# Folding the key weights of a linear-attention and FFN kernel in sixteen 32 by 32 array tiles, with block transpositions on VectorE in place of ScalarE copies

## The chip, the cores and the metric

The kernel runs on one NeuronCore of a Trainium2 chip. The metric is the device time of one execution in microseconds (us). Three executions of the kernel before took 513.17, 512.70 and 510.85 us, a median of 512.7. Beside these, one execution was profiled.

## The reference

A sigmoid gate, one number for each row of x, mixes two branches over the same input x of 2048 rows by 512 columns. Branch A is linear attention with 32 heads of 16 columns: queries and keys go through a small matrix per head (`w_phi`), then through a softmax of the result and one of its negative. Branch B is a feed-forward net with a squared ReLU. All is fp32.

```python
g = sigmoid((x * gate_w).sum(-1, keepdims=True))
q, k, v = split_heads(x @ wqkv)                       # 32 heads of 16
pq, pk = q @ w_phi[h], k @ w_phi[h]                   # per head
phi_q = concat(softmax(pq), softmax(-pq)); phi_k = concat(softmax(pk), softmax(-pk))
kv, z = phi_k.T @ v, phi_k.sum(rows)
a = (phi_q @ kv) / (phi_q @ z + 1e-6) @ wo
b = relu(x @ w1 + b1) ** 2 @ w2 + b2
out = g * a + (1 - g) * b
```

Since `x @ wk` is followed at once by `w_phi`, the kernel multiplies the two weight matrices first ("folds" them): `wk` (512 by 512) times a matrix that holds the 16 by 16 blocks of `w_phi` on its diagonal. Only the folded key weights, not the keys, are ever formed.

## The kernel before

**Precision.** Each fp32 product of the main work is three matmuls in a faster type: every operand is split into a high part (`hi`, a rounded copy, mostly by ScalarE) and a low part (`lo`, the difference, by VectorE), and `mm3` (L75 to L79) adds high by high, high by low and low by high. A matmul of this kind streams 512 columns. The fold is done in plain fp32 instead; there one matmul of the program gives two records in the trace.

**The FFN is the clockwork.** Its 14 chunks of 128 hidden columns run in two sweeps of seven over four blocks of 512 rows, 56 steps in all. A step is an `up` (12 matmuls into one PSUM bank `u`, then ReLU, square and split into `hh` and `hl`) and a `down` (12 matmuls, three for each of the four banks `d`). `up` runs two steps ahead of `down` (`LAG`). Each step has four slots, 2t, 2t + 0.5, 2t + 1 and 2t + 1.5; the last one stands between the second and the third `d` of a step. All attention work is hung into slots through `at(slot, function)`. The code sets the order in which work is offered; the scheduler orders each engine's queue by priority, `high_priority` pulls work ahead and `issue_after` fixes an order of two instructions.

**PSUM.** Four of the eight banks belong to `d`. The other four rotate: `bank()` hands out the one that was handed out longest ago, whoever asks: an `up`, a fold, a projection. A bank is written anew only when its last reader is done.

**Key and value weights.** Four tiles `raw[0]` to `raw[3]` of 128 by 1024 hold, for each quarter of the 512 input rows, the folded key weights beside the value weights; `raw[1]` and `raw[3]` lie in a tile named `tmp`. The value weights come by DMA (`joint_start`, L176); the folded ones come from PSUM. `joint(j, piece)` then makes of them the operands of seven products (the keys and values are computed by a scheme with seven block products in place of eight): subtractions on VectorE, and a split of each operand, into tiles named `slot...` and `w...`. Operands 1, 3 and 6 are stored to DRAM (`wkeep`) and loaded again later into the three slots by ScalarE's DMA queue (`again`, L556). The products `pX` and `pY` begin in slot 14 and read these operands.

**The fold.** `whole(k)` (L178 to L185) takes one bank, makes four 128 by 128 by 128 matmuls into its four quarters (input columns k of the transposed `wk`, held in four `row` tiles, by the diagonal `w_phi` matrix, in a fifth), and ScalarE copies the bank into `raw[k]` (L185). `joint(0, 0)` in slot 5 calls it for k = 0 and 2, `joint(1, 0)` in slot 6 for k = 1 and 3; after this one of the four banks (`ps_b`) leaves the rotation.

**Loads.** Weights and x come by SyncE's queue, which works in order. Weight and x tiles share four buffers (`stage`, tag `in`); a load waits until the split of the tile before it in that buffer is done. The gate's x tiles use the six `row` buffers, five of which hold the fold's inputs until the folds are done.

Of the kernel before, what the change touches and what calls it, by code (L numbers as in the profile page):

```python
# [10 lines left out]
AF = mybir.ActivationFunctionType  # L11
# [5 lines left out]
P = 128  # L17
S, D, H, DH, F = 2048, 512, 32, 16, 1792
NK = D // P
# [10 lines left out]
AHEAD = 150  # L30
# [5 lines left out]
def tile_gated_mix(ctx: ExitStack, tc: tile.TileContext, xT, xn, wqT, wkT, wphi, wv, wo, w1, b1, w2, b2, gw, out):  # L36
    nc = tc.nc
# [16 lines left out]
    def bank(name):  # L54
        p = banks[0]
        used(p)
        return p.tile([P, 512], F32, tag="s", name=name)
# [63 lines left out]
    st, up_w, down_w = {}, {}, {}  # L121
# [53 lines left out]
            st["raw"][k] = r  # L175
            nc.sync.dma_start(two(r)[:, :, 256:], two(wv[k * P:(k + 1) * P, :]))  # L176

    def whole(k):  # L178
        wph, *t = st["wT"]
        two = lambda a: a.rearrange("p (h c) -> p h c", h=2)  # L180
        ps = bank(f"fold{k}")
        for g in range(NK):
            nc.tensor.matmul(ps[:, g * P:(g + 1) * P], t[g][:, k * P:(k + 1) * P], wph[:, g * P:(g + 1) * P],
                             start=True, stop=True)
        nc.scalar.activation(two(st["raw"][k])[:, :, :256], two(ps), AF.Copy)  # L185

    def operand(i, j, src, slot=None, ehi=None, elo=None):
        if i in HELD:
# [9 lines left out]

    def joint(j, piece):
        raw, sub = st["raw"], lambda eng, o, a, b: eng.tensor_tensor(o, a, b, ALU.subtract)  # L200
        if piece == 0:
            whole(j)
            whole(2 + j)
        a, b = both(raw[j])
        c, d = both(raw[2 + j])
        if piece == 0:
            operand(3, j, d, j)
            operand(1, j, a, j)
            sub(nc.vector, a, b, a)
            sub(nc.vector, b, d, b)  # L210
        elif piece == 1:
            operand(5, j, a)
            operand(2, j, c)
            sub(nc.vector, a, d, a)
        else:
            operand(6, j, a, None if j else 2)
            sub(nc.vector, c, c, a)
            operand(7, j, b)
# [219 lines left out]
    def do_joint(j, piece):  # L438
        if (j, piece) == (0, 0):
            joint_start(st["wT"])  # L440
        with tc.issue_after(st["up"].ins):
            joint(j, piece)
        if (j, piece) == (1, 0):
            banks.remove(ps_b)
# [263 lines left out]
            at(2 * (fc - LAG) - 2, do_w1_first, fc)  # L708
        at(2 * (fc - LAG) - (2 if fc == LAG + 1 else 1), do_w2, fc)
    at(0, do_wT, wkT)  # L710
    for slot, j, piece in ((5, 0, 0), (6, 1, 0), (8, 0, 1), (9, 1, 1), (10, 1, 2), (11, 0, 2)):
        at(slot, do_joint, j, piece)
    for j in range(2):
        at(14.5, joint_last, j)
# [29 lines left out]
    for p in range(NB * NC // 2):  # L744
        n, s = 2 * p, 56.5 + 6 * p
        q, late = divmod(n, NC)[0], p == NB * NC // 2 - 1
# [13 lines left out]
    hid, last = {}, len(work_list) - 1  # L760
# [98 lines left out]
```

## Time and profile before

| | |
|---|---|
| three executions | 510.85, 512.70, 513.17 us |
| profiled execution, its time | 511.04 us |
| its span in the trace | 509.3 us (1.7 us lie around it) |
| granted TensorE clock | 0.999 |
| VectorE busy | 403.5 us (79%) |
| ScalarE busy | 254.8 us (50%) |
| fold of the key weights | PE 26.2 to 32.7 us, two blocks of 16 records |
| copies of L185 on ScalarE | 27.7 to 33.3 us, four of about 0.59 us |
| first `pX` | 54.31 us |

Times in rows of the trace are microseconds from the start of the span. A row of the timeline gives the start, the length, the engine, the line of the kernel, the operation, output and input tiles, the shape and the number of records merged; idle time of that engine before it stands in brackets with what ended it. A matmul's length includes its way through the array, so neighbours overlap, and what one costs is the distance between two starts: 0.227 us for the 512-column matmuls.

### The profile page before, as it was taken

The page shows a single profiled execution, that of the slowest core. Times are in us where ns is not written, and L with a number is a line of the kernel's source. Part 1 is how long each engine was busy: PE and PEld are TensorE (multiplying, and loading weights), DVE is VectorE, ACT ScalarE, POOL GpSimd, SP SyncE. Part 2 cuts the span into 40 slices and gives each one's busy share as a digit, 9 for nine tenths or more (in the row PEclk, how much of TensorE's full clock was granted, in tenths as well). Part 3 has the DMA queues.
Part 4 walks back from the last instruction along what each step waited for, and adds up shares of the span by engine and source line. Part 5 has one row for each costly group of instructions (what it writes and reads, how often), then busy time and mean ns, then how long its engine had stood idle before and what let it go on. Part 6 is the DMA issues. An engine that isn't in the chain of part 4 may idle for free.

```text
span 509.3 us, 9129 instructions
## 1 busy us (share of the span) xinstructions
PE 502.8 (99%) x3421; PEld 408.0 (80%) x3421; DVE 403.5 (79%) x668; ACT 254.8 (50%) x445; POOL 91.0 (18%) x106
## 2 busy tenths in 40 slices
PE   8999999999999999999999999999999999999997
PEld 4888888888788888788888878788787878788775
DVE  3559848888884979796998989897969797897723
ACT  4778645556253565463564744444456354333540
POOL 1001640204320024000012140211222120111200
PEclk9999999999999999999999999999999999999999
DMA  8975696667844478762266131324112231032112
GB/s 256 324 247 186 231 325 194 200 210 226 291 167 142 171 237 288 281 208 83 73 198 228 50 96 40 106 72 143 48 32 85 69 88 47 3 120 68 37 27 83
DMA packets 46628, 76.12 MB, mean 149 GB/s; under 512 B 6776, under 2 KB 23928, under 8 KB 46584
## 3 DMA queue, kind: packets, MB, share of 16 engines
q1 hardware_dynamic: 35544, 41.58, 26.5%
q10 hardware_dynamic: 8224, 24.51, 13.8%
q0 software_dynamic: 2816, 9.45, 5.1%
q8 instruction: 27, 0.44, 0.3%
q14 instruction: 17, 0.14, 0.1%
HBM read 57.68 MB, written 11.54 MB: 136 GB/s over the span
## 4 chain that ended last, share of the span: by engine, by line
PE 93%; DVE 3%; DMA 3%; issue 0%; DVEq 0%; ACT 0%
PE d L77 10%; PE d L78 9%; PE d L79 9%; PE u L77 9%; PE u L78 9%; PE u L79 9%; PE att L79 3%; PE att L78 3%; PE q L78 3%; PE q L77 3%; PE att L77 3%; PE q L79 3%; PE pX L579 3%; PE pX L577 2%; PE pX L578 2%; PE pY L577 2%
## 5 line engine op out<-in xcount | busy, mean ns | idle before, releaser
L407 ACT ACTIVATE r<-u,b1c 128x512 f32<-128x512 f32 x56 | 38.5, 687 | 125.3 <-PE u L79 123.8
L77 PE MATMUL d<-w2h,hh 128*128 128x512 f32 x224 | 87.8, 392 | 0.0
L78 PE MATMUL d<-w2l,hh 128*128 128x512 f32 x224 | 87.3, 390 | 0.0
L79 PE MATMUL d<-w2h,hl 128*128 128x512 f32 x224 | 87.2, 389 | 0.0
L77 PE MATMUL u<-xh,w1h 128*128 128x512 f32 x212 | 83.8, 395 | 0.0
L78 PE MATMUL u<-xl,w1h 128*128 128x512 f32 x212 | 82.6, 390 | 0.0
L79 PE MATMUL u<-xh,w1l 128*128 128x512 f32 x212 | 82.5, 389 | 0.0
L322 POOL TENSOR_TENSOR ez<-e,z 128x512 f32<-128x512 f32 x32 | 42.8, 1358 | 165.9 <-ACT e L294 165.9
L67 DVE TENSOR_TENSOR hl<-r,hh 128x512 fp32r<-128x512 f32 x56 | 37.7, 674 | 23.7 <-ACT hh L64 23.7
L77 PEld LDWEIGHTS d<-w2h,hh 128*128 128x128 f32 x224 | 42.1, 188 | 9.1 <-issue 0.4
L78 PEld LDWEIGHTS d<-w2l,hh 128*128 128x128 f32 x224 | 42.1, 188 | 8.9 <-DVE w2l L67 0.4
L79 PEld LDWEIGHTS d<-w2h,hl 128*128 128x128 f32 x224 | 42.1, 188 | 8.8
L77 PEld LDWEIGHTS u<-xh,w1h 128*128 128x128 f32 x212 | 39.8, 188 | 11.0 <-issue 3.1
L79 PEld LDWEIGHTS u<-xh,w1l 128*128 128x128 f32 x212 | 39.8, 188 | 8.4
L78 PEld LDWEIGHTS u<-xl,w1h 128*128 128x128 f32 x212 | 39.8, 188 | 7.8
L297 DVE TENSOR_REDUCE sm<-e 128x64 f32<-128x1024 f32 x27 | 32.8, 1213 | 11.1 <-ACT e L294 11.1
L294 ACT ACTIVATE e<-e 128x1024 f32<-128x1024 f32 x27 | 28.6, 1059 | 25.0 <-DVE e L292 24.7
L64 ACT ACTIVATE hh<-r 128x512 fp32r<-128x512 f32 x56 | 35.1, 627 | 0.9
L408 ACT ACTIVATE r<-r 128x512 f32<-128x512 f32 x56 | 34.9, 624 | 0.8
L360 ACT ACTIVATE phiT<-tb 32x256 f32<-32x256 f32 x64 | 26.4, 412 | 6.1 <-DVE tb L345 5.1
L329 DVE TENSOR_REDUCE dz<-ez 128x64 f32<-128x1024 f32 x16 | 19.4, 1210 | 11.6 <-POOL ez L322 11.6
L616 ACT ACTIVATE tmp<-pX 128x512 f32<-128x512 f32 x24 | 14.3, 597 | 27.3 <-PE pX L579 27.3
(171 smaller groups left out, 982.2 us busy)
## 6 DMA issues: line engine op xcount, KB each, us to landing
sloto<-wkeep ACTq DMA_DIRECT2D x30, 512.0 KB, 4.2
in<-in_xT SPq DMA_DIRECT2D x44, 256.0 KB, 3.7
slotez<-wkeep ACTq DMA_DIRECT2D x15, 512.0 KB, 4.5
phiT<-tb SPq DMA_DIRECT2D x192, 32.0 KB, 1.9
in<-in_w SPq DMA_DIRECT2D x23, 256.0 KB, 3.3
part<-row POOLq DMA_DIRECT2D x16, 256.0 KB, 5.0
row<-part SPq DMA_DIRECT2D x16, 256.0 KB, 3.1
out<-row SPq DMA_DIRECT2D x15, 256.0 KB, 2.2
```

Source lines behind the costliest of these rows:

```text
L64: i = nc.scalar.activation(hi, src, AF.Copy)
L67: st["lo"] = elo.tensor_tensor(lo, src, hi.bitcast(F32), ALU.subtract)
L77: nc.tensor.matmul(o, ah[:, sa], bh[:, sb], start=first, stop=False)
L78: nc.tensor.matmul(o, ah[:, sa], bl[:, sb], start=False, stop=False)
L79: return nc.tensor.matmul(o, al[:, sa], bh[:, sb], start=False, stop=last)
L294: nc.scalar.activation(ef, ef, AF.Exp)
L297: nc.vector.tensor_reduce(sm, e3, AX.X, ALU.add)
L322: nc.gpsimd.tensor_tensor(ez[:, hs, :], e3[:, hs, :], zbc[half], ALU.mult)
L360: nc.scalar.activation(dst, src, AF.Copy)
L407: st["relu"] = nc.scalar.activation(r, ps, AF.Relu, bias=b1c[:, fc:fc + 1])
L408: nc.scalar.activation(r, r, AF.Square)
L577: nc.tensor.matmul(ps, h, wh, start=first and j == 0, stop=False, skip_group_check=True)
```

## The change

`whole` goes. `tiles_fold` takes its place, once, in slot 5.5 in place of 5 and 6. It takes all four rotating banks at the same time and makes 64 matmuls of 32 by 32 (stationary: a 32 by 32 block of the diagonal `w_phi` matrix) by 128 columns (moving: the transposed `wk`). `r` picks the array's row tile and the bank, `c` its column tile, `g` the quarter of the bank; an order is fixed with `r` running fastest. The products are the same sums of 32 terms, of which 16 are not zero, but the result comes out transposed. So VectorE turns it: 16 block transpositions of 128 partitions by 128 elements, four per bank, straight from PSUM into the `raw` tiles, in a fixed order, bank by bank. The four copies on ScalarE are gone. Lines behind the change have moved by 11 to 14: L257 is now L268, L200 is L214, L577 is L590.

```diff
-    def whole(k):
-        wph, *t = st["wT"]
-        two = lambda a: a.rearrange("p (h c) -> p h c", h=2)
-        ps = bank(f"fold{k}")
-        for g in range(NK):
-            nc.tensor.matmul(ps[:, g * P:(g + 1) * P], t[g][:, k * P:(k + 1) * P], wph[:, g * P:(g + 1) * P],
-                             start=True, stop=True)
-        nc.scalar.activation(two(st["raw"][k])[:, :, :256], two(ps), AF.Copy)
+    def tiles_fold(loaded):
+        wph, *t = loaded
+        pss = [bank(f"fold{r}") for r in range(4)]
+
+        def mm(g, r, c):
+            rows, cols = slice(32 * r, 32 * r + 32), slice(32 * c, 32 * c + 32)
+            return nc.tensor.matmul(pss[r][cols, g * P:(g + 1) * P],
+                                    wph[rows, g * P + 32 * r:g * P + 32 * r + 32],
+                                    t[g][rows, :].rearrange("p (k c q) -> p k c q", c=4, q=32)[:, :, c, :],
+                                    start=True, stop=True, skip_group_check=True)
+
+        last = None
+        for x in [(g, r, c) for g in range(NK) for c in range(4) for r in range(4)]:
+            with tc.issue_after(last.ins) if last else nullcontext():
+                last = mm(*x)
+        turned = None
+        for r in range(4):
+            for k in range(NK):
+                src = pss[r].rearrange("p (h g k q) -> p h g k q", h=2, g=2, k=NK)[:, :, :, k, :]
+                dst = st["raw"][k].rearrange("p (h z g r f) -> p h z g r f", h=2, z=2, g=2, r=4)[:, :, 0, :, r, :]
+                with tc.high_priority(offset=AHEAD), tc.issue_after(turned.ins) if turned else nullcontext():
+                    turned = nc.vector.transpose(dst, src)
...
     def joint(j, piece):
-        if piece == 0:
-            whole(j)
-            whole(2 + j)
...
         if (j, piece) == (0, 0):
             joint_start(st["wT"])
+            with tc.issue_after(st["up"].ins):
+                tiles_fold(st["wT"])
...
-    for slot, j, piece in ((5, 0, 0), (6, 1, 0), (8, 0, 1), (9, 1, 1), (10, 1, 2), (11, 0, 2)):
+    for slot, j, piece in ((5.5, 0, 0), (6, 1, 0), (8, 0, 1), (9, 1, 1), (10, 1, 2), (11, 0, 2)):
```

How the queues of two engines change follows; `d_302` to `d_305` are the four banks of `down`, `w2h_262` and `w2h_268` the weights of the third and fourth step, `w1h_321`, `w1h_347` and `w1h_504` (before: `w1h_432`) the weights of the fifth, sixth and seventh chunk.

TensorE before, where the second half of the fold stands between a whole `down` and the `up` of the sixth chunk (the first half, `fold_397` and `fold_403`, stands right ahead of that `down`):

```order
L77 MATMUL d_305<-w2h_262,hh 128x512
L78 MATMUL d_305<-w2l_263,hh 128x512
L79 MATMUL d_305<-w2h_262,hl 128x512
L183 MATMUL fold_436<-row 128x128 x4
L183 MATMUL fold_442<-row 128x128 x4
L77 MATMUL u<-xh_0_145,w1h_347 128x512
L78 MATMUL u<-xl_0_146,w1h_347 128x512
```

TensorE after: the end of the 64 small matmuls, which now stand in one piece between the second and the third bank of that `down`. `fold_404` to `fold_407` are the four banks:

```order
L184 MATMUL fold_404<-row 32x128
L184 MATMUL fold_405<-row 32x128
L184 MATMUL fold_406<-row 32x128
L184 MATMUL fold_407<-row 32x128
L77 MATMUL d_304<-w2h_262,hh 128x512
L78 MATMUL d_304<-w2l_263,hh 128x512
L79 MATMUL d_304<-w2h_262,hl 128x512
```

TensorE after, ten rows behind the small matmuls (six for `d_304` and `d_305`, then these four), where the `up` of the sixth chunk begins:

```order
L77 MATMUL d_302<-w2h_268,hh 128x512
L78 MATMUL d_302<-w2l_269,hh 128x512
L79 MATMUL d_302<-w2h_268,hl 128x512
L77 MATMUL d_303<-w2h_268,hh 128x512
L77 MATMUL u<-xh_0_145,w1h_347 128x512
L78 MATMUL u<-xl_0_146,w1h_347 128x512
```

So the fold has moved six matmuls back, into one block, and four matmuls of the next `down` have moved ahead of the `up`; the other eight follow behind it, and then the `up` of the seventh chunk. The rotation gives that sixth `up` the bank `fold_405`, the second of the four, because the first leaves the rotation in between; it waits for VectorE's eighth transposition. The seventh `up` gets `fold_406`.

VectorE before, from the low part of the first x tile of the next block on:

```order
L67 TENSOR_TENSOR xl_0_459<-in,xh_0_458 128x512
L67 TENSOR_TENSOR sloto_388<-raw_393,sloto_388 128x512
L67 TENSOR_TENSOR xl_1_470<-in,xh_1_469 128x512
L67 TENSOR_TENSOR w_518<-raw_393,w_517 128x512
L67 TENSOR_TENSOR w2l_384<-in,w2h_383 128x512
L67 TENSOR_TENSOR sloto_389<-tmp,sloto_389 128x512
L67 TENSOR_TENSOR w1l_433<-in,w1h_432 128x512
```

VectorE after, the start of the transpositions behind the two x tiles:

```order
L67 TENSOR_TENSOR xl_0_519<-in,xh_0_518 128x512
L67 TENSOR_TENSOR xl_1_530<-in,xh_1_529 128x512
L199 STREAM_TRANSPOSE raw_398<-fold_404 128x2x2x32
L199 STREAM_TRANSPOSE tmp<-fold_404 128x2x2x32
L199 STREAM_TRANSPOSE raw_400<-fold_404 128x2x2x32
```

VectorE after, behind the last of them:

```order
L199 STREAM_TRANSPOSE tmp<-fold_407 128x2x2x32
L67 TENSOR_TENSOR w2l_384<-in,w2h_383 128x512
L67 TENSOR_TENSOR sloto_395<-raw_400,sloto_395 128x512
L67 TENSOR_TENSOR w1l_505<-in,w1h_504 128x512
L67 TENSOR_TENSOR sloto_396<-tmp,sloto_396 128x512
L67 TENSOR_TENSOR w_578<-raw_400,w_577 128x512
```

All 16 transpositions stand in one piece ahead of the splits of the next weights. The low part of the seventh chunk's weights, `w1l`, stands behind the split of a `raw` tile now, and so behind its high part on ScalarE. On every engine the order is the same again from the second `pX` on (about 67 us).

## The prediction

> **What bounds the kernel now.** I read the page first: the busy shares, then the chain that ended last by engine.
>
> ```profile
> span 509.3 us, 9129 instructions
> PE 502.8 (99%) x3421; PEld 408.0 (80%) x3421; DVE 403.5 (79%) x668; ACT 254.8 (50%) x445; POOL 91.0 (18%) x106
> PE 93%; DVE 3%; DMA 3%; issue 0%; DVEq 0%; ACT 0%
> ```
>
> The chain runs through TensorE for 93% of the span. So time is gained by taking work from TensorE's queue, and lost by a wait put into it. ScalarE is half idle: its four copies count only if something waits for them. Next comes the stage of the change, by the table of stages (columns: window, length, then busy time and records of PE, PEld, DVE, ACT and POOL, clock, DMA share, GB/s).
>
> ```profile
> 23.50:33.00 9.50, 9.50 (x59) 8.46 (x58) 5.58 (x10) 6.96 (x13) 0.57 (x1) 1.00 0.60 204
> 33.00:54.00 21.00, 21.00 (x94) 17.41 (x93) 17.78 (x32) 14.07 (x27) 4.45 (x6) 1.00 0.70 243
> ```
>
> TensorE has no gap here at full clock; VectorE is busy for 85% of the second window. Whatever goes onto VectorE can delay something. Last, TensorE's timeline around the fold.
>
> ```profile
> 26.00 0.39 PE L79 MATMUL u<-xh,w1l 128*128 128x512 f32 x1
> 26.23 1.95 PE L183 MATMUL fold<-row 128*128 128x128 f32 x16
> 27.93 0.48 PE L77 MATMUL d<-w2h,hh 128*128 128x512 f32 x1
> 28.25 0.40 PE L78 MATMUL d<-w2l,hh 128*128 128x512 f32 x1
> ...
> 30.75 1.95 PE L183 MATMUL fold<-row 128*128 128x128 f32 x16
> 32.45 0.48 PE L77 MATMUL u<-xh,w1h 128*128 128x512 f32 x1
> ...
> 37.99 0.39 PE L77 MATMUL u<-xh,w1h 128*128 128x512 f32 x1
> ...
> 38.44 0.39 PE L79 MATMUL u<-xh,w1l 128*128 128x512 f32 x1
> ```
>
> **Term 1, the fold on TensorE.** A block of 16 records holds the queue from 26.23 to 27.93, and the step to the next matmul is 0.32 in place of 0.23: 1.70 + 0.09 = 1.79. Two blocks: **3.58 us go**.
>
> The new block is 64 matmuls, 128 records at two each. The trace has no 32 by 32 tiles, but two relatives: L312 with four column tiles (the weight loads show its pace best) and L371 with two row by four column tiles.
>
> ```profile
> 111.27 0.39 PE L79 MATMUL d<-w2h,hl 128*128 128x512 f32 x1
> ...
> 111.59 0.61 PEld L312 LDWEIGHTS kvps<-e,vext 128*17 128x17 f32 x64 [0.35 <-DVE gate L264]
> 112.10 0.63 PEld L312 LDWEIGHTS kvps<-tmp,vext 128*17 128x17 f32 x64
> 112.78 0.19 PEld L577 LDWEIGHTS pY<-w,sh 128*128 128x128 f32 x1
> 112.89 0.19 PEld L578 LDWEIGHTS pY<-w,sh 128*128 128x128 f32 x1
> ```
>
> ```profile
> 492.07 1.09 PE L371 MATMUL num<-phiT,kvb 64*32 64x256 f32 x32
> 493.09 0.50 PE L77 MATMUL d<-w2h,hh 128*128 128x512 f32 x1
> ```
>
> L312 passes 128 records in 1.19 us (111.59 to 112.78), 9 ns each. Its neighbour would have followed 111.27 at 111.50, so 0.09 is lost on entry, and some 0.2 on leaving. Streaming alone is no higher: an old fold record takes 1.70/16 = 0.106 us, and 128 of them on 16 tiles are 0.85. I take L312's pace: 1.19 + 0.3 = **1.5 us come**. The ends: 0.85 + 0.3 = 1.15 below; above, L371's pace, 1.02 us for 32 records, so 4.1 + 0.3 = 4.4. TensorE's own work falls by about 2.1 us.
>
> **Term 2, the wait that is added.** The fold holds all four rotating banks, so the next `up`, ten matmuls behind it, waits for VectorE's eighth transposition. When do these begin? ScalarE and VectorE before:
>
> ```profile
> 27.15 0.63 ACT L408 ACTIVATE r<-r 128x512 f32<-128x512 f32 x1
> 27.69 0.58 ACT L185 ACTIVATE raw<-fold 128x512 f32<-128x512 f32 x1
> 28.16 0.62 ACT L64 ACTIVATE hh<-r 128x512 fp32r<-128x512 f32 x1
> ```
>
> ```profile
> 28.82 0.69 DVE L67 TENSOR_TENSOR hl<-r,hh 128x512 fp32r<-128x512 f32 x1 [1.61 <-ACT hh L64]
> 29.43 0.68 DVE L257 SCALAR_TENSOR_TENSOR row<-row,gwb 128x512 f32<-128x512 f32 x1
> ...
> 30.04 0.69 DVE L67 TENSOR_TENSOR xl<-in,xh 128x512 fp32r<-128x512 f32 x1
> ...
> 31.25 0.68 DVE L67 TENSOR_TENSOR xl<-in,xh 128x512 fp32r<-128x512 f32 x1
> ```
>
> The copy at 27.69 stood ahead of `hh`; without it `hh` starts when `r` is done, near 27.81, and `hl` near 28.47. Then come the gate's row and two x tiles at 0.605 each: the first transposition starts at 28.47 + 4 x 0.605 = 30.89, with the fold finished at 26.23 + 6 x 0.227 + 1.4 = 29.0. So not the fold but VectorE's queue sets the start. Price of one transposition of 128 elements from PSUM, which the trace doesn't have:
>
> ```profile
> 342.19 1.24 DVE L345 STREAM_TRANSPOSE tb<-e 128x1024 f32<-128x1024 f32 x1
> 343.35 0.65 DVE L289 TENSOR_REDUCE mx<-q 128x32 f32<-128x512 f32 x1
> ```
>
> ```profile
> 12.49 0.69 DVE L495 TENSOR_TENSOR w1l<-row,w1h 128x128 fp32r<-128x128 f32 x3
> 13.10 0.68 DVE L67 TENSOR_TENSOR w1l<-row,w1h 128x512 fp32r<-128x512 f32 x1
> ```
>
> ```profile
> L680 DVE COPY kvb<-kvt x4: 279/286/298, 258.1 to 261.1; 32x128 f32<-32x128 f32 x4
> ```
>
> Three operations of 128 elements take 0.61 from start to start, 0.20 each. The 1024-element transposition takes 1.16; ordinary ones go by 0.605 for 512 and 0.20 for 128, so 1.05 ns an element and 0.07 fixed, 1.14 for 1024. It costs 0.02 to 0.03 more, so 0.23 each. Lower end 0.20; upper end 0.29, the full length of a PSUM copy of 128 elements, if nothing overlaps; and, far off, 0.60, if small blocks cost what 512 elements cost. By 0.23 the eighth is done at 30.89 + 8 x 0.23 + 0.13 (the tail of the last and the signal) = 32.86. TensorE gets there at 27.59 + 1.5 + 10 x 0.227 = 31.36 and waits **1.5 us**. Its whole queue stands behind that wait: this `up`, the rest of the `down`, the seventh `up`; ScalarE's ReLUs wait for these, but their results are used two steps later.
>
> The Trainium skill, VectorE: DVE Perf Modes, The three transpose paths, gives 311 ns for a 128x128 bf16 transpose on VectorE. If that held from start to start, the eighth would be done at 33.5 and the whole change would come to -0.05 us, 511.1; the trace's 1.24 us long row starts its successor 0.08 before its end, so I hold that figure for a length.
>
> **Net.** The `up` after that starts 20 matmuls later, at 32.86 + 20 x 0.227 = 37.40; before, at 37.99. So **0.6 us** is gained (3.58 - 1.5 - 1.5, the same).
>
> **What else moves.** The seventh `up` needs `w1h` and, in its third matmul, `w1l`:
>
> ```profile
> 36.59 0.63 ACT L64 ACTIVATE w1h<-in 128x512 fp32r<-128x512 f32 x1 [1.94 <-DMA in<-in_w]
> 37.26 0.69 DVE L67 TENSOR_TENSOR w1l<-in,w1h 128x512 fp32r<-128x512 f32 x1 [1.80 <-ACT w1h L64]
> ```
>
> Its load waits for the second x tile's buffer. That tile was done at 31.93; now it is done at 30.97, so at the old latency the tile lands near 35.6, by 1.0 earlier. `w1l` now stands behind a high part (0.52) and a low part (0.6): 35.6 + 0.6 + 0.5 + 0.7 + 0.7 = 38.1 at worst, against a need at 37.40 + 0.45 = 37.85. SyncE's two gate loads now go ahead of it, but no store of a slot competes. I take no wait; bound 0.25. The sixteen transpositions take 3.7 and end at 34.7. VectorE idled 21.00 - 17.78 = 3.2 us in the window from 33 to 54, 1.80 of it right ahead of that `w1l`, so its backlog at the window's end is about the old one; if that cover were gone, the first `pX` would be late by 0.5 at most. ScalarE's four copies (the one above takes 0.58, so 2.3 us) I cost at nothing: it idles half the time.
>
> Around 56 to 77 us ScalarE's queue changes too: a reload of the first slot now stands behind a copy of `pX` that came at 66.07.
>
> ```profile
> 62.68 0.33 ACTq L565 DMA_DIRECT2D sloto<-wkeep  x1
> ...
> 66.07 0.60 ACT L616 ACTIVATE tmp<-pX 128x512 f32<-128x512 f32 x1 [2.28 <-PE pX L579]
> ...
> 70.25 0.33 ACTq L565 DMA_DIRECT2D sloto<-wkeep  x1
> ```
>
> ```profile
> 76.75 0.39 PE L577 MATMUL pX<-sloto,xh 128*128 128x512 f32 x1
> ```
>
> ```profile
> DMA to landing us min/median/max: 3.7/4.2/5.5
> ```
>
> ```profile
> 124.01 4.49 DMA sloto<-wkeep
> ```
>
> The line on landing counts the slot loads between 50 and 80 us; the last row is a piece of the chain. So this 512 KB load leaves 3.4 us later and lands by 71.6, beside POOL's loads, and still runs when the next one leaves at 70.25. That one is needed by `pX` at 76.75, and at 5.5 us has 1.0 left. I take 0; the far end is 0.6, all that was gained.
>
> **Sum.** 511.04 - 0.6 = 510.4 for the profiled execution. It lies 1.7 below the median of 512.7; the four known executions have their middle at 511.9. I predict 511.9 - 0.6 = **511.3**.
>
> **Rivals.**
> 1. *The gain is given back at the slot reloads.* For: the chain holds such a load, of 4.49 us, further on, and the moved one falls into busy traffic. Against: 1.0 us left. Time: no change, 511.9 (511.0 on the profile's basis).
> 2. *Slower: the transpositions cost more.* The deciding point is 0.305 us each (37.99 - 4.54 - 30.89 - 0.13, by eight); above it the bank wait outweighs the fold. For: block work straight from PSUM, unseen here. Against: 0.20 and 1.16. At 0.60 each the bank comes free at 35.8 (loss 2.4) and `w1l` is ready near 42.6 (loss 4.1): 516.0. The Trainium skill, TensorEngine Tiling (Array Packing), PSUM Bottleneck, says that tiles speed up TensorE and not the emptying of PSUM, which may become the bottleneck. By that rule this rival or the forecast's 1.5 us wait is what to expect; no run so far shows which.
> 3. *The tiles don't run side by side as hoped.* At L371's pace the block is 4.4: the fold ends at 31.9, the eighth transposition at 33.9, TensorE arrives at 34.3: loss 0.9, 512.8. One after another (128 x 0.106 = 13.6) would lose 10. Against: L371 does run eight tiles at once, 32 records of about 0.21 in 1.02.
> 4. *The wait doesn't bind* and the 2.1 us stay: 509.8. It would need transpositions that start 1.5 us earlier; nothing in the queue allows it.
>
> **How the numbers follow.** Chances: forecast (gain 0.3 to 0.9) 0.5; rival 1 0.22; rival 2 0.14, of which 0.05 dear enough for over 0.5%; rival 3 0.07; rival 4 0.07. About 0.5%, 2.6 us, is what a measurement of this kernel can tell from no change. Even the whole 2.1 is under it, so faster is left to rival 4 and a lucky scatter of the runs, 0.07; slower has 0.05 of rival 2, 0.02 of rival 3 and 0.03 of scatter, 0.10; the rest, 0.83, lies within. Low end: the fastest execution 510.85 less 1.2; high end: the slowest, 513.17, plus 0.7 for rivals 2 and 3: 509.6 to 513.9.
>
> **What would show it.** Right: one block of 128 fold records of 1.2 to 1.6 us; transpositions 0.2 to 0.3 apart from about 30.9; a TensorE gap of 1 to 2 us, released by VectorE, ahead of the sixth `up`; the seventh `up` at 37.2 to 37.7. Wrong: no gap there (rival 4), a gap at `w1l` or a step over 0.3 (rival 2), a fold block over 3 us (rival 3), a new gap at `pX` near 76 (rival 1).

## The result and the profile after

The changed kernel took 514.51 us (median of 7 runs, 513.54 to 516.17), the kernel before 511.47 (7 runs beside it, 510.85 to 513.17): ratio 1.0057, 95% interval 1.0043 to 1.0071, so **slower by 3.0 us**. 511.3 was predicted. The profiled execution of the changed kernel took 513.54, 2.5 more than that of before.

First the page of the changed kernel: span, busy times, the chain by engine, and the queue that brings instructions (packets, MB, share).

```profile
span 511.7 us, 9331 instructions
PE 502.2 (98%) x3517; PEld 405.4 (79%) x3517; DVE 406.2 (79%) x684; ACT 253.3 (49%) x441; POOL 91.4 (18%) x106
PE 68%; issue 13%; DVE 7%; DMA 5%; ACT 2%; POOL 2%; SPq 1%; DVEq 0%; POOLq 0%; ACTq 0%
q8 instruction: 28, 0.46, 0.4%
```

TensorE is busy for 0.6 us less, and the span is 2.4 longer: TensorE waits. Before, the chain ran through it for 93%; now for 68%. The page of before has 27 packets on the last line, not 28.

The waits of TensorE (total, times, longest), without those at the start and at `kvps`, which both kernels have:

```profile
PE d L77 <- DVE row L822: 1.6, 1, 1.6
...
PE pX L592 <- issue: 0.7, 1, 0.7
...
PE u L77 <- DVE tmp L199: 0.7, 1, 0.7
...
PE num L382 <- DMA phiT<-tb: 0.4, 1, 0.4
```

Only the third of these was forecast. The others lie at 61, 212 and 303 us. TensorE's and VectorE's timeline at the fold:

```profile
27.55 1.90 PE L184 MATMUL fold<-row 32*32 32x128 f32 x128
...
32.62 0.47 PE L77 MATMUL u<-xh,w1h 128*128 128x512 f32 x1 [0.67 <-DVE tmp L199]
...
37.25 0.39 PE L77 MATMUL u<-xh,w1h 128*128 128x512 f32 x1
```

```profile
30.77 0.31 DVE L199 STREAM_TRANSPOSE raw<-fold 128x128 f32<-128x128 f32 x1
...
33.78 0.27 DVE L199 STREAM_TRANSPOSE tmp<-fold 128x128 f32<-128x128 f32 x1
```

Here the change does what was forecast: the seventh `up` starts at 37.25 in place of 37.99. To see where the gain goes, the same matmul is followed through both traces. The table gives, for every profiled execution, how much later than in the first profile of before the same `down` matmul starts, as the growth of that offset in each stage; stages are named by their times in before. "Load" is when ScalarE starts the high part `w2h` near 34 us, which waits for a weight load. The kernels below the third row are explained with the experiments.

| profile | start | fold, 23 to 41 | 41 to 52 | block end, 52 to 71 | 71 to 194 | 194 to 249 | 249 to 325 | load |
|---|---|---|---|---|---|---|---|---|
| after | -0.13 | -0.60 | 0.00 | +1.96 | 0.00 | +0.49 | +0.75 | 33.80 |
| after_again | -0.07 | +0.08 | 0.00 | +2.23 | +0.19 | +1.36 | +0.74 | 35.12 |
| after_third | -0.12 | -0.24 | 0.00 | +2.09 | +0.76 | +1.51 | +0.27 | 34.51 |
| before_again | +0.71 | 0.00 | 0.00 | +0.02 | +1.05 | -0.19 | +0.05 | 34.20 |
| load_only | -0.06 | +0.08 | +1.44 | 0.00 | -0.07 | -0.14 | -0.28 | 35.62 |
| tile_only | -0.23 | -1.09 | +1.51 | +1.14 | +0.99 | +1.05 | +0.81 | 34.37 |
| order_back | -0.04 | -0.64 | 0.00 | +2.05 | +0.05 | +0.80 | +1.31 | 33.97 |
| later_w4 | +0.21 | -0.62 | 0.00 | +1.75 | -0.06 | +0.52 | +0.57 | 33.82 |
| old_order | -0.26 | -0.04 | 0.00 | +1.05 | +0.64 | +0.98 | -0.05 | 34.22 |
| less_vec | -0.06 | +0.72 | 0.00 | +1.45 | -0.07 | +1.06 | +0.50 | 35.73 |
| two_step_l | +0.53 | -1.44 | +1.13 | +0.65 | -0.07 | +3.29 | +0.68 | 34.43 |
| phase_after | +0.02 | +0.39 | +0.01 | +2.01 | +0.41 | 0.00 | -0.31 | 35.53 |
| mid_after | +0.56 | +0.30 | 0.00 | +1.85 | +0.96 | 0.00 | -0.32 | 35.83 |
| later_w4_phase | +0.63 | +0.08 | 0.00 | +1.24 | +0.50 | -0.52 | -0.11 | 35.79 |
| old_order_mid | -0.14 | -0.19 | 0.00 | +1.48 | +1.15 | -0.53 | -0.28 | 34.78 |
| two_step_lp | +0.11 | -0.79 | +1.42 | +0.69 | +0.49 | -0.46 | -0.28 | 35.02 |
| two_step_rp | +0.07 | -0.79 | +1.55 | +0.05 | +2.13 | +0.01 | -0.17 | 34.97 |
| phase_before | +2.29 | +0.02 | +0.11 | 0.00 | +0.30 | +1.24 | +0.85 | 35.95 |
| mid_before | +0.29 | 0.00 | 0.00 | 0.00 | +5.43 | +1.26 | +0.62 | 33.78 |

The first row sums to +2.5, the difference of the two times. One profile is one execution: between 71 and 194 us a second profile of the unchanged kernel loses 1.05, 0.7 of it a wait of `pX` for a slot reload, so only what comes back in several profiles is read here. The gain at the fold, 0.60, was predicted at 0.59. It is lost three times over at the end of the first block, and some more at two places where the engines' orders are the same in both kernels.

**The block end.** There VectorE finishes the gate (L268 to L276) and then adds the first `d` banks to the output (L822), which frees them for the next block's `down`. VectorE and ScalarE after:

```profile
54.12 0.69 DVE L268 SCALAR_TENSOR_TENSOR row<-row,gwb 128x512 f32<-128x512 f32 x1
54.73 0.09 DVE L268 DVE_READ_ACCUMULATOR row<-row,gwb 128x1 f32 x1
54.73 1.22 DVE L67 TENSOR_TENSOR hl<-r,hh 128x512 fp32r<-128x512 f32 x1
55.87 1.22 DVE L67 TENSOR_TENSOR w<-raw,w 128x512 fp32r<-128x512 f32 x1
57.02 0.70 DVE L274 TENSOR_SCALAR gate<-gate 128x4 f32<-128x4 f32 x1
57.63 0.68 DVE L67 TENSOR_TENSOR w<-tmp,w 128x512 fp32r<-128x512 f32 x1
58.23 0.16 DVE L275 RECIPROCAL gate<-gate 128x4 f32<-128x4 f32 x1
58.43 0.50 DVE L276 TENSOR_SCALAR rest<-gate 128x4 f32<-128x4 f32 x1
58.85 1.45 DVE L67 TENSOR_TENSOR sl<-in,sh 128x512 fp32r<-128x512 f32 x2
60.22 0.75 DVE L822 SCALAR_TENSOR_TENSOR row<-d,rest,row 128x512 f32<-128x512 f32 x1
```

```profile
56.63 0.60 ACT L629 ACTIVATE tmp<-pX 128x512 f32<-128x512 f32 x1 [1.58 <-DMA wkeep<-spare]
57.72 0.63 ACT L64 ACTIVATE sh<-in 128x512 fp32r<-128x512 f32 x1 [0.49 <-POOL in L560]
58.94 0.63 ACT L64 ACTIVATE sh<-in 128x512 fp32r<-128x512 f32 x1 [0.59 <-POOL in L561]
59.48 0.71 ACT L813 ACTIVATE row<-b2b,rest 128x512 f32<-128x512 f32 x1
```

From the end of the gate's row (54.81) to the end of the first evacuation (60.97) pass 6.2 us. A second profile of the unchanged kernel shows the same place with VectorE just as late:

```profile
54.08 1.22 DVE L257 SCALAR_TENSOR_TENSOR row<-row,gwb 128x512 f32<-128x512 f32 x1
55.23 0.08 DVE L257 DVE_READ_ACCUMULATOR row<-row,gwb 128x1 f32 x1
55.58 0.34 DVE L263 TENSOR_SCALAR gate<-gate 128x4 f32<-128x4 f32 x1 [0.27 <-ACT gate L262]
...
57.54 0.75 DVE L809 SCALAR_TENSOR_TENSOR row<-d,rest,row 128x512 f32<-128x512 f32 x1 [0.79 <-ACT row L800]
```

Here it is 3.0 us (55.31 to 58.29), as in the first profile of before, and TensorE loses 0.02. So the changed kernel has another order there: `hl` and the two splits of the last operand `w` stand between the gate's steps, two `sl` ahead of the evacuation; and on ScalarE the `row` copy that the evacuation needs stands behind a slot reload that waits for a store and behind two `sh` that wait for GpSimd's sums. The same place in the first profile of before, VectorE and then TensorE:

```profile
53.70 0.08 DVE L257 DVE_READ_ACCUMULATOR row<-row,gwb 128x1 f32 x1
...
56.01 0.75 DVE L809 SCALAR_TENSOR_TENSOR row<-d,rest,row 128x512 f32<-128x512 f32 x1 [0.79 <-ACT row L800]
```

```profile
59.75 0.39 PE L77 MATMUL d<-w2h,hh 128*128 128x512 f32 x1
```

TensorE after:

```profile
61.02 0.50 PE L77 MATMUL d<-w2h,hh 128*128 128x512 f32 x1 [1.61 <-DVE row L822]
```

In before the gate's row ended at 53.78 and the first evacuation at 56.76, 3.0 ahead of TensorE's need at 59.75. After: 1.0 late at the gate's row, 3.2 more behind it, TensorE there 0.7 earlier: 1.0 + 3.2 + 0.7 - 3.0 = 1.9, and the table has 1.96. The same sum from the rows of the other profiles gives 2.0 for `after_again` and `after_third` (table: 2.23 and 2.09), 2.0 for `phase_after` (2.01), 1.8 for `mid_after` (1.85), 0.9 for `tile_only` (1.14) and less than nothing for `before_again` and `load_only` (0.02 and 0.00). It holds where the first evacuation is what TensorE waits for; in `old_order` it is not.

### The profile page after: what moved, and what is told of

Its sections match the earlier page's. It is cut to its first block, busy times and chain, and to the rows that moved or that the text cites. A ratio compares the mean times of both kernels' runs of the same rounds, so it can differ in the third digit from the quotient of the medians.

```text
span 511.7 us, 9331 instructions
## 1 busy us (share of the span) xinstructions
PE 502.2 (98%) x3517; PEld 405.4 (79%) x3517; DVE 406.2 (79%) x684; ACT 253.3 (49%) x441; POOL 91.4 (18%) x106
## 4 chain that ended last, share of the span: by engine, by line
PE 68%; issue 13%; DVE 7%; DMA 5%; ACT 2%; POOL 2%; SPq 1%; DVEq 0%; POOLq 0%; ACTq 0%
PE d L77 7%; PE d L78 7%; PE d L79 7%; PE u L77 6%; PE u L78 6%; PE u L79 6%; PE att L79 3%; PE att L78 3%; PE att L77 3%; PE q L79 2%; PE q L78 2%; PE q L77 2%; PE pX L592 2%; PE pX L591 2%; PE pX L590 2%
```

## The experiments

Three explanations were set against each other. **Sum**: the loss at 52 to 71 is VectorE's lateness plus the order at the block's end (called LOAD and ORDER where only one is meant). **Phase**: the losses at 212 and 303 come from the fold's 128 records in place of 32, 96 more, which shift the places where packets of the instruction queue (the `q8` line above) arrive in TensorE's work. The rival to both was that the tiles or the transpositions themselves are dear.

### The parts of the change

`tile_only`: the 64 small matmuls, with ScalarE copying the 16 pieces; the transposition is left out.

```diff
-                    turned = nc.vector.transpose(dst, src)
+                    turned = nc.scalar.activation(dst, src, AF.Copy)
```

> The changed kernel with the transpositions left out: ScalarE copies the sixteen 128x128 pieces from the four banks as they stand, so the key weights enter the rest with each 32 by 32 block not transposed. TensorE's new fold alone, without VectorE's 3.2 us of transpositions. The order at the end of the first block stays the changed one (the high and low parts of key weight 4 ahead of the gate's small steps, both `sh` and `sl` ahead of the row copies and of the first d evacuation). Theory LOAD (VectorE's 3.2 us are what makes the first d of the second block wait): no wait there, the fold's 1.7 us stay, 509.8. Theory ORDER (the changed order on VectorE and ScalarE near 55 us makes it wait, whatever the load): a wait of 1 to 2 us before that d remains, 511.0 to 512.0. Theory FOLD (the 128 tile records themselves cost TensorE more later): 513 or more.

515.44 us, ratio 1.0065 (1.0049 to 1.0081). LOAD and ORDER both missed: the kernel is slower even without a transposition on VectorE. FOLD alone had such a time (513 or more), and the table shows where it goes: the fold itself gains 1.09, then `xl` is late by 1.2 near 46 us, the block end costs 1.14, and 1.05 and 0.81 are lost at 212 and 303, where the added records are the suspect.

`load_only`: the kernel before, with its four copies on VectorE in place of ScalarE.

```diff
-        nc.scalar.activation(two(st["raw"][k])[:, :, :256], two(ps), AF.Copy)
+        nc.vector.tensor_copy(two(st["raw"][k])[:, :, :256], two(ps))
```

> The kernel before with its four fold copies moved from ScalarE to VectorE, nothing else: 4 x 0.605 = 2.4 us more on VectorE at the same place, the old fold on TensorE, and an order at the end of the first block that is the old one but for three of the four row copies, which now stand behind `sh`. Theory LOAD: VectorE is late at the block's end by 1 to 2 us and the first d of the second block waits, 512.5 to 513.5. Theory ORDER: that d's evacuation had 3.0 us to spare before, the load takes at most 2.4 of them, no wait, 511.2 to 511.9.

512.54, ratio 1.0006 (0.9993 to 1.0018): no difference. Its last gate row starts at 54.05, as late as after the change, and the block end loses nothing. The profile shows one wait at 46 us:

```profile
PE u L78 <- DVE xl L67: 1.2, 1, 1.2
```

So VectorE's load alone is not what makes the block end late, though it can make `xl` late.

`less_vec`: the changed kernel without two of the four gate rows of each block (those gates are left out).

```diff
+        if n in (1, 2):
+            return
```

> The changed kernel with the gate rows of tokens' chunks 1 and 2 of the first block left out (their gate columns keep the zero set at the start): 1.2 us less on VectorE between 40 and 49 us. Theory QUEUE (whatever the order, the end of the first block follows VectorE's queue, which is 1.0 us late there): the last gate row ends near 53.6, the loss between 58 and 66 us falls from 1.96 to 0.7 to 1.0, total 513.3 to 513.6. Rival ORDER: the loss stays, 514.2 or more.

514.54, ratio 1.0066 (1.0045 to 1.0086). The loss fell to 1.45 only, and the load came at 35.73, so VectorE was late all the same (last gate row from 54.95). It decides nothing.

### The order at the block's end

`later_w4` offers the last operand's splits later:

```diff
-        at(14.5, joint_last, j)
+        at(16, joint_last, j)
```

> The changed kernel with one half of that only: the split of key weight 4 is listed at slot 16, the row copies stay behind `sh`. Theory ORDER: the gate's three small steps now follow the last gate row, some 2 us earlier, but the first row copy still waits for both `sh` and these for POOL's sums (58.9 us); the wait before d shrinks only as far as these sums end earlier without VectorE beside them: 513.6 to 514.5. Theory LOAD: 514.2 to 514.8.

514.25, ratio 1.0045 (1.0027 to 1.0063). The wait of `d` falls from 1.6 to 0.9; the evacuation still stands behind the two `sl`. Of the loss of 1.75 the sum above gives 1.2; the rest comes later, with a `pX` that waits 0.2 for a slot reload at 70 us.

Both of the next two have `later_w4`'s edit. `order_back` adds priority for all four `row` copies of the first block's end, `old_order` for the first alone (shown):

```diff
-                nc.scalar.activation(o, b2b, AF.Copy, scale=rest[:, n:n + 1])
+                with tc.high_priority(offset=AHEAD) if b == 0 and c == 0 else nullcontext():
+                    nc.scalar.activation(o, b2b, AF.Copy, scale=rest[:, n:n + 1])
```

> The changed kernel with the order at the first block's end put back: the split of key weight 4 is listed at slot 16 in place of 14.5, and the first block's four row copies get the priority of the evacuations, so that they stand ahead of `sh`. The fold and the sixteen transpositions stay. Theory ORDER: the first d of the second block finds its bank free, the 1.96 us lost between 58 and 66 us come back, 514.5 - 2.0 = 512.5. Theory LOAD: VectorE's last gate row is still 1.0 us later and POOL's sums too, so at least 1.2 us of the wait stay, 513.7 or more.

514.92, ratio 1.0058 (1.0040 to 1.0076). A miss: the evacuations are in time, but now `sh` and `sl` stand behind four copies, and `pX` waits for them (0.9 and 0.5): 2.05 lost as before, at another tile.

> The changed kernel with the split of key weight 4 listed at slot 16 and only the first of the four row copies raised in priority, so that ScalarE goes row copy, `tmp`, `sh`, `sh`, other rows, and VectorE goes gate steps, first d evacuation, `sl`, as before the change (order_back raised all four rows, and `sh` then came too late). Theory SUM (the wait is the sum of two parts: VectorE's last gate row is 1.0 to 2.2 us later than before, and the new order puts 3.2 us more between that row and the first d evacuation; before had 3.0 us to spare there): with the second part gone the first alone is covered, the loss between 58 and 66 us falls from 2.0 to 0.5 or less, 1.5 us faster than after_third. Rival QUEUE (whatever the order, TensorE comes out of the block end as late as VectorE's gate row is): the loss stays at 1.2 or more, at most 0.7 us faster.

513.46, ratio 1.0034 (1.0018 to 1.0049). 4.2 us from gate row to evacuation in place of 6.2, the loss 1.05 in place of 2.0 to 2.2. The first evacuation is in time; the second `d` waits 0.7 for its own. With the same order `old_order_mid` below loses 1.48, so a quarter to a half of the block-end loss goes with the order, with the transpositions in place. The result lies between the two theories: 1.0 us less than `after_third`, where SUM wanted 1.5 and QUEUE (the end follows VectorE's lateness whatever the order) at most 0.7.

### The shift of the instruction stream

At 212 TensorE stops inside a block of `pX`, released by nothing that the trace shows ("issue"): in the profile of after, the matmul that starts at 211.77 follows one of 210.66, its weight load started at 210.67, and the trace names nothing that it waits for. `phase_after` is the changed kernel with 64 more TensorE instructions, tiny matmuls put in place of a part of the warm-up; `phase_before` shifts the unchanged kernel's stream in the same way, by as much as the change does; `later_w4_phase` is `later_w4` with the 64.

```diff
-        idle(11)
+        idle(10)
+        z = st["zeros"]
+        for _ in range(33):
+            st["up"] = nc.tensor.matmul(st["warm"][:8, :8], z[:, :8], z[:, :8], start=True, stop=True)
```

> The changed kernel with one wide warm-up matmul replaced by 33 of 8 by 8, in the idle time ahead of the first w1h: 32 records or 64 instructions of TensorE more, so that with the 192 of the new fold its instruction stream is longer by 256 than before, which is the number between two of its instruction fetches as the traces show them. The order of all else is that of the changed kernel. Theory PHASE (beside the 2 us lost between 58 and 66 us, some 1.3 us are lost because the fold's other number of records shifts TensorE's instruction fetches: a stop without releaser inside a `pX` block at 211 us, and a SyncE issue of 2.45 us at 292.7 that makes `num` wait at 303): both go, the fetches fall where they did before, 514.5 - 1.3 = 513.2. Rival CHANCE (those two are scatter of single executions or come from the new order): they stay or move, 514.2 to 514.8.

514.05, ratio 1.0057 (1.0043 to 1.0070). The stop and the wait of `num` are gone from the profile, but the time is that of the changed kernel. In the profiled execution the load was late and the fold lost 0.39; whether that explains the median isn't shown.

> The kernel before with six wide warm-up matmuls replaced by 102 of 8 by 8: 96 records or 192 instructions of TensorE more, the same shift as the new fold's, with the old fold and the old order. PHASE: the stop inside `pX` near 209 and the `num` wait near 302 appear in this kernel too, 512.0 + 1.0 to 1.5 = 513.0 to 513.5. CHANCE: neither appears, 511.6 to 512.4.

514.99, ratio 1.0082 (1.0054 to 1.0111). +1.24 at 214 and +0.85 behind, as foretold, but the shorter warm-up also cost 2.29 at the start (the first three `up` matmuls take 1.62 us in place of 0.93): the time says nothing, the two steps do.

> The split of key weight 4 listed at slot 16 and the 64 more TensorE instructions together. If the two act apart: later_w4's 514.25 less the stop at 211 (0.5) and what else the fetches cost it (0.5 at 260): 513.2 to 513.8. If PHASE is wrong: 514.0 to 514.5.

513.53, ratio 1.0047 (1.0033 to 1.0061). No stop and no wait of `num`. The time is in the range foretold, but beside the kernel before in the same set the ratio is no lower than `later_w4`'s 1.0045.

So that the warm-up stays as it is, `mid_after` puts 16 tiny matmuls (32 records) between two halves of `kvps` at 139 us; `mid_before` puts 48 into the unchanged kernel there. Both kernels were run again beside them.

```diff
+            for _ in range(16 if p == 2 else 0):
+                with tc.issue_after(later.ins):
+                    later = nc.tensor.matmul(st["kv"][:8, 256:264], ident[:, :8], ident[:, :8], start=False, stop=False,
+                                             skip_group_check=True)
```

> The kernel before once more, for a second profiled execution of it beside those of this set: ratio 1.000 within 0.1%. Read against the first profile it says which of the small TensorE gaps belong to the kernel and which to one execution. PHASE expects no stop inside `pX` near 210 and no `num` wait near 302 here too.

511.13, ratio 1.0000 (0.9990 to 1.0011).

> The changed kernel once more, on the same chip as the two below: 1.0057 of the kernel before within 0.15%. PHASE expects the stop inside `pX` near 211 and the `num` wait near 303 again; CHANCE expects them to be gone or elsewhere. QUEUE expects the loss between 58 and 66 us again, about as large as VectorE's last gate row is late.

515.25, ratio 1.0076 (1.0063 to 1.0090), a little above the range expected. The stop is 1.5 us here:

```profile
PE d L77 <- DVE row L822: 1.6, 1, 1.6
PE pX L592 <- issue: 1.5, 1, 1.5
...
PE u L77 <- DVE tmp L199: 1.2, 1, 1.2
```

> The changed kernel with 16 matmuls of 8 by 8 (32 records, 64 instructions) put between the two halves of `kvps` at 139 us, into unused columns of its bank; all else in the same order. From there on TensorE's instruction fetches fall where they fell before, and nothing ahead of 139 us is touched, the warm-up neither. PHASE: 0.2 us come there, the stop at 211 and the num wait at 303 go: 1.0 to 1.3 us faster than after_again. CHANCE: no faster.

514.29, ratio 1.0059 (1.0047 to 1.0072). TensorE's longest waits in the profile:

```profile
PE d L77 <- DVE row L826: 1.5, 1, 1.5
PE u L77 <- DVE tmp L199: 1.2, 1, 1.2
```

`pX` and `num` are off the list. The kernel is 0.96 us faster than `after_again`, about as forecast, though the pad itself costs 0.7.

> The kernel before with 48 such matmuls (96 records, 192 instructions) at the same place: the shift that the new fold brings, from 137 us on. The warm-up, which phase_before cut short so that its first matmuls ran slower, stays whole. PHASE: 0.5 us for the records and 1.0 to 1.5 for the stop inside `pX` and the num wait: 1.003 to 1.004 of before. CHANCE: 1.001.

518.27, ratio 1.0151 (1.0121 to 1.0181). The pad cost far more than was reckoned, 5.4 us. A stop of 1.4 lies in it, and behind that stop TensorE's granted clock, the column ahead of the last two, is at half for 3.4 us:

```profile
144.00:146.00 2.00, 2.00 (x6) 1.52 (x6) 0.00 (x0) 0.00 (x0) 0.00 (x0) 0.50 0.00 0
```

Six matmuls fill the 2 us there, 0.43 from start to start in place of 0.227; by that pace the stretch costs some 1.6 of the 5.4. All six executions of this kernel have such a low mean clock (0.989 to 0.997). Behind the pad come +1.26 at 213 to 217 and +0.62 at 303. The wait at 217 is put down to a weight load here, as is that of `phase_before`, so that it is the same stop is likely, not shown.

The window from 205 to 218 us by queues gives the instruction packets there: two in the changed kernel, one in `mid_after`.

```profile
q8 instruction: 2, 0.03, 1.0%
```

```profile
q8 instruction: 1, 0.02, 0.8%
```

On average there is one such packet for 251 TensorE instructions, matmuls and weight loads (7034 make 28). To half a microsecond, two of them lie 4.0 us apart around the stop in the profiles of after, after_again and two_step_l (209.0 and 213.0 in the first); in before, mid_after and two_step_lp, without the stop, 11 to 12 us apart (197.5 and 209.5 in the first). Closeness alone doesn't make a stop: two packets lie as close at 138.5 and 143.0 in before and at 232.5 and 237.0 in after, and TensorE doesn't stop there. The wait of `num` is a late SyncE issue: a DMA issue that falls on a packet (292.0) takes 2.45 us. Timeline of SyncE after:

```profile
292.26 0.38 SPq L87 DMA_DIRECT2D in<-in_xT  x1
292.74 2.45 SPq L365 DMA_DIRECT2D phiT<-tb  x1
```

In the table's column 194 to 249, the nine profiles with the change's 96 records and no pad have +0.49 to +3.29 (the largest, `two_step_l`, with 3.4 us at half clock behind its stop of 1.8), the two padded kernels of before +1.24 and +1.26, and the nine with the old phase (the first profile of before, at 0, among them) +0.01 or less.

`after_third` and `old_order_mid` (`old_order` with the pad of `mid_after`) repeat the comparison with `old_order`'s order.

> The changed kernel again, as the reference on this chip for the two below: 1.0057 to 1.0076 of the kernel before.

514.44, ratio 1.0051 (1.0033 to 1.0069), a little below the range expected.

> That order and the 16 small TensorE matmuls at 139 us of mid_after together. SUM and PHASE: both losses go, 2.3 to 2.8 us faster than after_third, 1.001 to 1.003 of the kernel before. QUEUE: 1.0 to 1.7 us faster.

513.36, ratio 1.0028 (1.0017 to 1.0039), no stop. Over `old_order` it gains 0.1, with a pad that costs 0.6. Over `after_third` it gains 1.1: that is QUEUE's range, not the 2.3 to 2.8 that SUM and PHASE together foretold.

### Both causes taken away

`two_step_l`: ScalarE empties the banks with sixteen copies into a scratch tile, VectorE transposes from there with four instructions of 512 elements; the last operand is late as in `later_w4`. `two_step_lp` adds the warm-up's 64 instructions, `two_step_rp` priority for the first two `row` copies as well.

```diff
+                    copied = nc.scalar.activation(dst, src, AF.Copy)
...
-                    turned = nc.vector.transpose(dst, src)
+                turned = nc.vector.transpose(dst, to.rearrange("p (h c) -> p h c", h=2))
```

> The changed kernel with the transposing put in two steps: ScalarE empties the four banks with sixteen copies of 128 elements into a scratch tile, VectorE transposes from there with four instructions of 512 elements; the last slot combinations stay late as in later_w4. The copies are 0.155 apart on ScalarE (tile_only), so the banks come free near 32 us and the transpositions cost VectorE 4 x 0.6 = 2.4 in place of 3.2. SUM theory (VectorE's 3.2 us in the fold stage, with the order at the block's end, cost the 2 us at 58 to 66): no bank wait over 0.3, VectorE's last gate row 0.5 to 1 us earlier than in the changed kernel, loss at the block's end under 1.0. PHASE theory: the 96 additional records are still there, so a stop of 0.6 to 1.5 at 211 to 217 and a wait of num at 303 remain. Time: 1.001 to 1.004 of before. Rival (only the order at the block's end counts, not VectorE's load): as later_w4, 1.0045.

514.17, ratio 1.0045 (1.0032 to 1.0058), the rival's figure.

> two_step_l with 64 more TensorE instructions in the warm-up, of the same length (as in later_w4_phase). PHASE theory: no stop at 211 to 217 and no wait of num at 303, all else as in two_step_l, so 0.9 to 1.9 us less than two_step_l: 0.997 to 1.002 of before. If the instruction stream's shift does not matter: as two_step_l.

513.03, ratio 1.0026 (1.0014 to 1.0037). It is 1.1 us faster than `two_step_l`, as foretold; the ratio is above the range.

> two_step_lp with the first two row copies of the block's end put early on ScalarE (as one row in old_order). SUM theory: both first d rows are evacuated in time, and the waits at 58 to 66 fall under 0.7 in all; 0.997 to 1.002 of before. If sh and sl behind the rows become the wait (as in order_back): 0.5 to 1.5 more than two_step_lp.

513.42, ratio 1.0037 (1.0024 to 1.0051), above its range too, though the block end is nearly free of loss.

VectorE of `two_step_lp`, in the fold stage and at the block's end:

```profile
31.14 1.30 DVE L204 STREAM_TRANSPOSE raw<-flat 128x512 f32<-128x512 f32 x2
32.36 1.26 DVE L204 STREAM_TRANSPOSE tmp<-flat 128x512 f32<-128x512 f32 x2
35.68 0.69 DVE L67 TENSOR_TENSOR w2l<-in,w2h 128x512 fp32r<-128x512 f32 x1 [2.06 <-ACT w2h L64]
...
54.60 0.68 DVE L273 SCALAR_TENSOR_TENSOR row<-row,gwb 128x512 f32<-128x512 f32 x1
...
58.66 0.75 DVE L830 SCALAR_TENSOR_TENSOR row<-d,rest,row 128x512 f32<-128x512 f32 x1 [0.79 <-ACT row L821]
```

The bank wait is gone in all three, VectorE's transpositions take 2.5 in place of 3.2 us, and the block end loses 0.05 to 0.69. But the step saved on VectorE turns into idle time ahead of `w2h` (2.06 us), the last gate row is no earlier than after the change (54.0 to 54.7 against 54.1), and a wait stands at `xl` near 46 us, 0.8 to 1.2 long, as in `load_only` and `tile_only`, which takes back what the fold gains:

```profile
PE u L78 <- DVE xl L67: 1.1, 1, 1.1
...
PE d L77 <- DVE row L830: 0.4, 1, 0.4
```

So a third place remains, and why `xl` is late there isn't settled. `two_step_lp` is slower than the kernel before and faster than the changed kernel, which was measured at 1.0057, 1.0076 and 1.0051; only against the first two do the intervals lie apart. No version here beats that one.

## Why the prediction was wrong

**The fold (term 1)** held in kind. The block is 128 records; the matmul behind it starts at 29.39, 1.84 after 27.55, and with entry and exit some 2 us come in place of 1.5, inside the range of 1.15 to 4.4. Streaming side by side is real: 14 ns a record, where an old fold record took 106. The excess doesn't show in the net, because TensorE would otherwise have waited longer for the bank.

**The bank wait (term 2)** is there, at the `up` and with the releaser forecast: 0.67 in the profile, 0.3 to 1.2 in the other kernels with these transpositions, against 1.5. The transpositions begin at 30.77 (forecast 30.89) and come every 0.20 us (forecast 0.23), at the lower bound. The 311 ns that the prediction weighed (the Trainium skill, VectorE: DVE Perf Modes, The three transpose paths) is near the 0.27 to 0.31 us of one row's length here, in fp32 from PSUM; it is not the step from start to start. (The 511.1 that the prediction gives for that case stands on the profiled execution's 511.04; on the forecast's own basis it would be 511.95.) The rule on emptying PSUM (the Trainium skill, TensorEngine Tiling (Array Packing), PSUM Bottleneck) has the bank wait of 0.3 to 1.2 beside it here: it applies, but it decides neither the sign nor the size of the result. In `after_again` the wait is 1.15, because an earlier weight load is late, and with it the ReLU behind that split on ScalarE, `hl`, and the transpositions behind it. ScalarE and VectorE in `after_again`, where the rows of after have 24.52 and 30.77:

```profile
25.66 0.63 ACT L64 ACTIVATE w2h<-in 128x512 fp32r<-128x512 f32 x1 [2.52 <-DMA in<-in_w]
...
26.85 0.67 ACT L418 ACTIVATE r<-u,b1c 128x512 f32<-128x512 f32 x1
```

```profile
31.31 0.31 DVE L199 STREAM_TRANSPOSE raw<-fold 128x128 f32<-128x128 f32 x1
```

**The net of 0.6 at the seventh `up`** was right to a tenth for the profiled execution; in the other two it is 0.24 gained and 0.08 lost, so that hit is in part the luck of one execution. In `after_third` the bank wait is the same 0.67, and the rest goes at the seventh `up`'s third matmul, which waits for `w1l`, the wait that the prediction took as none with a bound of 0.25. It starts 0.25 late there:

```profile
37.21 0.69 DVE L67 TENSOR_TENSOR w1l<-in,w1h 128x512 fp32r<-128x512 f32 x1
```

```profile
37.95 0.50 PE L79 MATMUL u<-xh,w1l 128*128 128x512 f32 x1
```

So even the gain that was right locally is not one of every execution. Whether the old kernel would bear a load as late isn't shown: where its loads were late (before_again, phase_before), TensorE had started late by about as much.

**The step that failed** is "What else moves": that VectorE's "backlog at the window's end is about the old one; if that cover were gone, the first `pX` would be late by 0.5 at most". Two things are wrong in it. The cover was partly not usable: VectorE's 3.2 us of idle time in that window lie ahead of splits that wait for a weight load. Before, it split two key weights while it waited; now the folded weights are only there when the transpositions are done, so VectorE idles for the load (0.42 us, and 1.05 for a high part that stands behind the next load on ScalarE) and splits afterwards. The gate's last row comes 1.0 late. And what is late next is not `pX` but the evacuation of `d`. That lateness alone is harmless (load_only and before_again have it), and the new order alone would cost 3.2 + 0.7 - 3.0 = 0.9; together they cost 2.0. The prediction read the order up to the seventh `up` and the slot reloads of 56 to 77 us, and not VectorE's and ScalarE's rows around the gate at 54 to 61, which stand in another order though the change edits none of them.

**The second miss**, a cost that had no step at all: 96 more records shift TensorE's instruction stream. In the profiles that is 0.5 to 1.5 us at 212 and 0.3 to 0.8 at 303, and it goes with a pad, or comes with one in the kernel before. In the timed runs it is less clear: the five pairs with and without a pad differ by 0.0000, 0.0017, -0.0002, 0.0006 and 0.0019 of the time, pads included, 0.4 us in the mean. That a pad takes the stop away is settled, and that it brings the same stop into the kernel before is likely; what it is worth in the median stays open, and so does what makes TensorE stop there and not at other packets that lie as close. Why the weight loads land up to 1.3 us apart in the same kernel (33.80 to 35.12) is open too.

**The rivals.** Rival 1 (slot reloads) did not decide: `pX` waits for one by 0.2 to 1.9 us in some executions of both kernels and of variants, and in the profile of after not at all. Rival 2 named the right sign for a wrong reason, since the transpositions were cheap: 0.20, under its deciding point of 0.305. Rivals 3 and 4 did not come. The mechanism behind the largest loss (a gate chain that is late and in another order) was no rival at all, and the chance of 0.10 for slower rested on prices alone.

## What to carry to other kernels

A change in one stage of a list-scheduled kernel re-orders engines that it doesn't touch: compare the order of every engine up to the point where both are the same again, and price every place ahead of that point, above all chains of short steps such as a gate. Idle time of an engine is cover only if the work to be covered is ready when the idle time is there; ask what that time waits for. A local gain under a microsecond can be right and still vanish, so follow one and the same matmul through both traces and take more than one profile.

## What the runs showed of the hardware

- On sixteen 32 by 32 tiles the fold's fp32 matmuls of 128 columns ran at 14 ns a record (1.84 us for 128).
- VectorE and GpSimd slow each other: `hl` and `w` took 1.22 in place of 0.68 us while GpSimd's sums ran (54.73 and 55.87 after), and of these sums, L559 and L560 took 1.07 beside such work, 0.74 in before, where VectorE ran only the gate's short steps and evacuations.
- The number of TensorE instructions ahead of a place can decide whether TensorE stops there for 0.6 to 1.8 us, with the same orders and the same data; and a SyncE DMA issue that met an instruction packet took 2.45 us (292.74 after), where one of the same line at 290.48 took 0.59.
- Tiny matmuls used as padding are not free: 48 of them cost 5.4 us in `mid_before`, 1.4 of it a stop and some 1.6 a stretch of 3.4 us at half the granted clock; 16 cost 0.7 in `mid_after`.
- A stop of TensorE of under 2 us can be followed by half the granted clock for 3.4 us (`two_step_l`, stop of 1.8; `mid_before`, 1.4), and need not be (`after_again`, 1.5).
